# Six batches of queries on GpSimd's DMA queue, in place of keys cast by that queue: retention and a gated convolution on one core

## The chip, the cores and the metric

The kernel runs on one core of a Trainium2 chip. The metric is the time of one execution on the device in microseconds (us); the lower the better. The engines go by the profile's names: PE is TensorE (PEld its weight loads), DVE VectorE, ACT ScalarE, POOL GpSimd, SP SyncE. A DMA can be issued from SP's queue (the profile's "hardware_dynamic" q1) or from POOL's ("software_dynamic" q0); the same 16 DMA engines carry both.

## The reference

Inputs are q, k and v, each 8 batches x 8 heads x 576 tokens x 64 in f32, and the weights of a gated unit over 512 channels. The output is 8 x 576 x 512 in f32.

```python
# retention
scores = (1/sqrt(D)) * q @ k^T                        # per batch and head, 576 x 576
gamma  = 1 - 2 ** (-5 - h)
ret    = scores * where(i >= j, gamma[h] ** (i - j), 0)
attn   = ret @ v
# gated unit, on x = attn with the heads side by side (8 x 576 x 512)
gate   = sigmoid(sum over 5 taps of conv_w[tap] * x shifted by tap)   # causal, per channel
out    = (gate * (x @ w_val)) @ w_out
```

## The kernel before

The tokens are cut into 36 chunks of 128: in each half of the batches (four of them) 16 full chunks, four to a batch, and two "tail" chunks, each of the last 64 tokens of two batches. Within a chunk the scores are taken directly under a triangular mask; all earlier chunks of the batch come in through a running state (`state`, the sum of k^T v). The decay is split into a factor on v (`gin`, put on when v is rounded to bf16) and one on the result (`gout`).

The schedule is written out by hand: a loop over steps t from -2 to 37 emits each engine's instructions in the order in which that engine will run them. What one step emits for the change:

- `load(t + 6)`: DMA issues on SP's queue. `load_one` brings one chunk in f32, 256 KB in pieces of 256 B (64 floats of one head and token). Before the change it brings the values of every chunk, the keys of chunks 0 to 3 only, and the tails' own queries.
- `load_queries(b)`: one DMA of 1 MB on SP's queue for the queries of the four full chunks of batch b, in pieces of 1 KB (four tokens of one head), into the tile `fqb` of two buffers. Batches 0 and 1 are loaded ahead of the loop; for the others the step stands in `qload`.
- `load_keys(t + 6)`: a DMA on POOL's queue that reads 256 KB of f32 keys and writes 128 KB of bf16 straight into `kb`, which has 11 buffers; all chunks from the fifth (chunk 4) on go this way, chunk 4 ahead of the loop.
- `cast_v(t + 2)` (line 217): POOL multiplies the values by `gin` and rounds them, `vb`, four buffers. `cast_k` (line 212) rounds the first four chunks' keys, on DVE for chunks 0 and 1, on POOL for 2 and 3. `cast_q` (line 230) rounds one chunk's worth of queries on POOL, one step ahead of its transposition.
- TensorE's work of a step: `scores(t + 1)` (L275), `values(t)` (L316), `turn_k(t + 2)`, which transposes the keys (L237, read from `kb`), `turn_q` (L237 from `qb`), for every second step the convolution (L380) and the value product (L395), for the others the output projection (L406), and at the end `carried(t + 1)` (L299) and `update(t + 1)` (L347), the state update, which reads `kb` and `vb`.
- In odd steps SP issues two output DMAs (line 412), each of which waits for ACT's copy out of PSUM (line 409). SP issues in order, so what comes behind waits too.

Of the kernel before, what the change touches and what calls it, by code (L numbers as in the profile page):

```python
# [13 lines left out]
F32 = mybir.dt.float32  # L14
BF16 = mybir.dt.bfloat16
# [6 lines left out]
def kernel(  # L22
# [10 lines left out]
    nc = tc.nc  # L33
    B, H, S, D = q.shape
    DM = moe_w_val.shape[0]
    KC = moe_conv_w.shape[0]
    P = 128
    NP = H // 2
    NCH = S // P
    TAIL = S - NCH * P  # L40
    PAD = KC - 1
    GB = 4
    LA = 8
    RQ = NCH
# [5 lines left out]
    half = ctx.enter_context(tc.tile_pool(name="half", bufs=2))  # L50
    bfp = ctx.enter_context(tc.tile_pool(name="bfp", bufs=4))
# [12 lines left out]
    chunks = []  # L64
# [4 lines left out]
    NT = len(chunks)  # L69

    with tc.manual_schedule():
# [3 lines left out]
        def load_one(name, src, kind, b, c, bufs):  # L75
            t = half.tile([P, H, D], F32, name=f"f{name}c", bufs=bufs)
            if kind == "full":
                nc.sync.dma_start(out=t, in_=src[b, :, c * P:(c + 1) * P, :].rearrange("h p d -> p h d"))  # L78
            else:
                for i in range(2):  # L80
                    nc.sync.dma_start(out=t[i * TAIL:(i + 1) * TAIL],
                                      in_=src[b + i, :, c * P:S, :].rearrange("h p d -> p h d"))
            loaded[name, kind, b, c] = t

        def load(t):
            kind, b, c = chunks[t]
            if t < NCH:
                load_one("k", k, kind, b, c, NCH)
            if kind == "tail":
                load_one("q", q, kind, b, c, 2)  # L90
            load_one("v", v, kind, b, c, LA + 1)

        def load_keys(t):

            kind, b, c = chunks[t]
            kb = bfp.tile([P, H, D], BF16, name="kb", bufs=LA + 3)
            if kind == "full":
                nc.gpsimd.dma_start(out=kb, in_=k[b, :, c * P:(c + 1) * P, :].rearrange("h p d -> p h d"))  # L98
            else:
                for i in range(2):  # L100
                    nc.gpsimd.dma_start(out=kb[i * TAIL:(i + 1) * TAIL],
                                        in_=k[b + i, :, c * P:S, :].rearrange("h p d -> p h d"))
            kbf[t] = kb

        kbf, vbf = {}, {}

        def load_queries(b):
            t = half.tile([P, H, RQ, D], F32, name="fqb", bufs=2)
            nc.sync.dma_start(out=t.rearrange("p h r d -> p h (r d)"),
                              in_=q[b, :, 0:RQ * P, :].rearrange("h (p r) d -> p h (r d)", r=RQ))  # L110
            loaded["qb", b] = t

        cwn = consts.tile([KC * NP, P], F32, name="cwn")
        nc.scalar.dma_start(out=cwn, in_=moe_conv_w.rearrange("k (o i) -> (k o) i", i=P))
        load_one("k", k, *chunks[0], NCH)
        load_queries(0)
        load_one("v", v, *chunks[0], LA + 1)
        load(1)
# [60 lines left out]
        nc.vector.tensor_tensor(id2, ident[:, 0:64], ident[:, 64:128], op=ALU.add)  # L179
        mask_t = consts.tile([P, P], BF16, name="maskt")  # L180

        load_keys(NCH)

        wvb = consts.tile([P, NP, NP, P], BF16, name="wvb")
        wob = consts.tile([P, NP, DM], BF16, name="wob")
        dg = consts.tile([P, NP, KC, 64], BF16, name="dg")
# [20 lines left out]
            copy(wob[:, o], wof[:, o])  # L207


        def cast_k(t):  # L210
            kb = bfp.tile([P, H, D], BF16, name="kb", bufs=LA + 3)
            (nc.vector if t < 2 else nc.gpsimd).tensor_copy(kb, loaded["k", *chunks[t]])  # L212
            kbf[t] = kb

        def cast_v(t):
            vb = bfp.tile([P, H, D], BF16, name="vb")
            nc.gpsimd.tensor_tensor(vb, loaded["v", *chunks[t]],  # L217
                                    gin[:, chunks[t][2], :].unsqueeze(2).to_broadcast([P, H, D]), op=ALU.mult)
            vbf[t] = vb
# [4 lines left out]
        def cast_q(job, eng=nc.gpsimd):  # L224
            qb = bfp.tile([P, H, D], BF16, name="qb", bufs=5)
            if job[0] == "own":
                src = loaded["q", *chunks[job[1]]]
            else:
                src = loaded["qb", job[1]][:, :, job[2], :]
            eng.tensor_copy(qb, src)  # L230
            qbf[job] = qb
# [10 lines left out]
        def turn_k(t):  # L242
            ps = turned(kbf[t])
            kt = tp_sb.tile([P, NP, P], BF16, name="kt")
            nc.vector.tensor_copy(kt, ps)  # L245
            ktd[t] = kt

        def turn_q(job, copy=nc.scalar.copy, pool=None):
            ps = turned(qbf[job], pool)
            if job[0] == "own":  # L250
                qt = tp_sb.tile([P, NP, P], BF16, name="qt")
                qtd["own", job[1]] = qt
                dst = qt
            else:
                b, r = job[1:]
                if r == 0:
                    qtd["batch", b] = tp_sb.tile([P, NP, RQ, P], BF16, name="qtb", bufs=2)
                dst = qtd["batch", b][:, :, r, :]
            copy(dst, ps)  # L259
# [126 lines left out]
        def gate(n, i):  # L386
            t = gp.tile([P, 2, 2 * P], F32, name=f"gate{i}")
            nc.scalar.activation(t, gps[n][i], AF.Sigmoid)  # L388
            gsb[n].append(t)
# [28 lines left out]
        ok = lambda t: 0 <= t < NT  # L418
# [9 lines left out]
        qload = {}  # L428
        for b in range(2, B):
            first = min(s for s in qjobs if ("batch", b, 0) in qjobs[s])  # L430
            qload.setdefault(max(0, first - LA + 2), []).append(b)

        v_copy, g_copy, s_copy = nc.vector.tensor_copy, nc.gpsimd.tensor_copy, nc.scalar.copy
        for t in range(-2, NT + 2):
            n = t // 2 - 1
            unit = 0 <= n < NT // 2
            odd = t % 2 == 1
            jobs = qjobs.get(t, [])
            if t == -2:

                cast_k(0)
                turn_k(0)
                for s in sbl:
                    nc.vector.memset(s, 0.0)
                for r in range(RQ):
                    cast_q(("batch", 0, r), nc.vector if r % 2 else nc.gpsimd)
                cast_v(0)
                for r in range(RQ):
                    turn_q(("batch", 0, r), s_copy if r % 2 else v_copy, ps_g if r < 3 else None)
                warm = consts.tile([P, 1], F32, name="warm")  # L450
                nc.scalar.activation(warm, lsc, AF.Sigmoid)
                continue
            for b in qload.get(t, []):
                load_queries(b)
            if t >= 0 and ok(t + LA - 2):
                load(t + LA - 2)
            if ok(t + 2) and t == -1:
                cast_k(t + 2)
            if ok(t + 2):
                cast_v(t + 2)  # L460
            if t == -1:
                prep_wv(g_copy, 0)
            if t + 3 < NCH:
                cast_k(t + 3)
            if t >= -1 and NCH <= t + LA - 2 < NT:
                load_keys(t + LA - 2)
            for job in qjobs.get(t + 1, []):
                cast_q(job)
            if ok(t):
                take_state(t)  # L470
            if ok(t + 1):
                scores(t + 1)
                masks(t + 1, 0)
            if ok(t):
                values(t)
                if not odd:
                    take_x(t)
            if ok(t + 1) and not odd:
                masks(t + 1, 1)
            if unit and not odd:  # L480
                conv(n)
                gate(n, 0)
                gate(n, 1)
            if ok(t + 2) and not 1 <= t <= 3:
                turn_k(t + 2)
            if ok(t) and odd:
                take_x(t)
            if ok(t + 1) and odd:
                masks(t + 1, 1)
            if t == -1:  # L490
                prep_conv_weights()
            early = jobs if not 1 <= t <= 3 else []
            if unit:
                project(n, 0) if odd else value(n, 0)
            for job in early:
                turn_q(job)
            if unit:
                project(n, 1) if odd else value(n, 1)
            if ok(t + 2) and 1 <= t <= 3:
                turn_k(t + 2)  # L500
                for i, job in enumerate(jobs):
                    turn_q(job, v_copy if i % 2 else s_copy)
            if ok(t + 1):
                carried(t + 1)
                update(t + 1)
            if -1 <= t <= 0:
                prep_diagonals(2 * t + 2)
                prep_diagonals(2 * t + 3)
            if t == 1:
                prep_wv(s_copy, 1)  # L510
            if t == 2:
                for o in range(NP):
                    prep_wo(s_copy if o % 2 else v_copy, o)
                nc.gpsimd.tensor_copy(mask_t, mask)
                nc.gpsimd.memset(mask_t[0:64, 64:128], 0.0)
# [29 lines left out]
```

## Time and profile before

| | us |
|---|---|
| times of three runs | 176.56, 177.33, 178.78 |
| median | 177.33 |
| the profiled execution's own time | 176.56 |
| its span in the profile | 174.7 |

| engine | busy us | share of the span |
|---|---|---|
| PE | 150.4 | 86% |
| DVE | 117.7 | 67% |
| POOL | 94.1 | 54% |
| ACT | 88.4 | 51% |

| DMA issued | from | count, KB each | median us to landing |
|---|---|---|---|
| `fqb` (queries of a batch) | SP | 8 x 1024 | 9.0 |
| `fvc` (values of a full chunk) | SP | 32 x 256 | 6.9 |
| `fkc` (keys of the first chunks) | SP | 4 x 256 | 6.8 |
| `kb` (keys, cast; bytes written) | POOL | 28 x 128 and 8 x 64 | 7.2 and 4.6 |
| output | SP | 32 x 256 | 4.2 |

The profile comes from one execution, and the span is the part of its time from the first to the last thing that the profiler saw. Busy time is a mean over a start of some 24 us, in which the first loads arrive, and a steady run after it. "L98" is line 98 of the kernel. A DMA engine can work on packets of two queues at once, so shares of DMA time can add to more than 100%. In the lines of an engine in order of time, the numbers are the start and the length in us, and in brackets the idle time before and what ended it; in the list of waits they are the total, the number and the longest.

### The profile page before, as it was taken

The numbers are of one execution on the slowest core, as the hardware profiler recorded it, in microseconds if no ns is written. First come the engines' busy times: TensorE is split into PE (matmuls) and PEld (weight loads), VectorE is DVE, ScalarE is ACT, GpSimd is POOL, SyncE is SP. The second block draws the span as 40 slices with busy tenths as digits, with TensorE's granted clock in tenths as the row PEclk, the third lists the DMA queues.
The fourth block names the chain that finished last, engine by engine and source line by source line (L and its number), as shares of the span: only waits on it lengthen the run. The fifth ranks groups of instructions, "written<-read, shape, count | busy, mean of one in ns | idle before, by whom it ended". The sixth has DMA issues, their size and how long they took to land.

```text
span 174.7 us, 5491 instructions
## 1 busy us (share of the span) xinstructions
PE 150.4 (86%) x2273; PEld 111.9 (64%) x2273; DVE 117.7 (67%) x229; ACT 88.4 (51%) x180; POOL 94.1 (54%) x123
## 2 busy tenths in 40 slices
PE   0275359489999999999999999999999999999980
PEld 0154247357786868677686868677786867777630
DVE  6667813476767777776867777776866788776330
ACT  6361412175566565647454565647475554545330
POOL 7256257469994597825970795578575243100000
PEclk9999999999999999999999999999999999999998
DMA  5999999999999999999999999999999991303114
GB/s 136 279 293 249 219 261 233 298 283 221 249 292 254 226 223 199 283 183 294 178 271 237 220 300 244 198 246 203 161 185 123 230 219 64 120 4 123 71 50 120
DMA packets 93957, 36.00 MB, mean 206 GB/s; under 512 B 80090, under 2 KB 88302, under 8 KB 93934
## 3 DMA queue, kind: packets, MB, share of 16 engines
q1 hardware_dynamic: 60400, 31.20, 70.2%
q0 software_dynamic: 33344, 4.20, 37.7%
q8 instruction: 17, 0.28, 0.7%
q10 hardware_dynamic: 190, 0.27, 0.6%
q14 instruction: 6, 0.05, 0.1%
HBM read 30.42 MB, written 9.44 MB: 228 GB/s over the span
## 4 chain that ended last, share of the span: by engine, by line
PE 80%; SPq 9%; DMA 4%; DVE 2%; ACT 1%; issue 1%; POOL 0%; ACTq 0%; DVEq 0%
PE g L395 19%; PE g L406 17%; PE g L380 13%; PE tps L237 11%; PE o L316 7%; PE s L275 6%; SPq L78 4%; DMA fkc<-in_k_dram 4%; PE st L347 4%; SPq L125 3%; PE o L299 3%; SPq L121 1%; DVE z L398 1%; ACT qtb L259 1%; ACT ob L409 1%
## 5 line engine op out<-in xcount | busy, mean ns | idle before, releaser
L217 POOL TENSOR_TENSOR vb<-fvc,gin 128x512 bf16<-128x512 f32 x36 | 37.6, 1045 | 36.2 <-DMA fvc<-in_v_dram 12.8
L284 DVE TENSOR_TENSOR p<-s,maskq 128x512 bf16<-128x512 f32 x64 | 43.8, 685 | 15.1 <-PE s L275 14.9
L398 DVE TENSOR_TENSOR z<-gate,g 128x512 bf16<-128x512 f32 x36 | 24.8, 688 | 20.9 <-PE g L395 20.9
L395 PE MATMUL g<-xg,wvb 128*128 128x256 bf16 x288 | 37.4, 276 | 0.0
L406 PE MATMUL g<-wob,z 128*128 128x512 bf16 x144 | 36.3, 379 | 0.3 <-DVE z L398 0.3
L409 ACT COPY ob<-g 128x512 f32<-128x512 f32 x36 | 21.1, 586 | 25.7 <-PE g L406 25.5
L388 ACT ACTIVATE gate<-g 128x512 f32<-128x512 f32 x36 | 19.5, 594 | 20.0 <-PE g L380 20.0
L395 PEld LDWEIGHTS <-wvb 128*128 128x128 bf16 x288 | 27.0, 99 | 3.7 <-issue 0.8
L98 POOL DMA_DIRECT2D kb<-in_k_dram x28 | 26.6, 948 | 0.0
L358 ACT CAST sbd<-st 64x256 bf16<-64x256 f32 x48 | 17.6, 367 | 16.6 <-PE st L347 16.1
L237 PE MATMUL tps<-ident,kb 128*128 128x128 bf16 x144 | 15.1, 231 | 11.1 <-POOL kb L212 6.5
L380 PE MATMUL g<-xg,dg 64*64 64x256 bf16 x720 | 24.3, 279 | 0.0
L230 POOL CAST qb<-fqb 128x512 bf16<-128x512 f32 x30 | 19.1, 643 | 8.6 <-DMA fqb<-in_q_dram 8.6
L326 DVE TENSOR_TENSOR xg<-o,gout 128x512 bf16<-128x512 f32 x32 | 21.7, 680 | 0.0
L259 ACT COPY qtb<-tps 128x512 bf16<-128x512 bf16 x27 | 15.9, 589 | 9.2 <-PE tps L237 9.2
L380 PEld LDWEIGHTS <-dg 64*64 64x64 bf16 x720 | 19.0, 109 | 2.3 <-issue 0.6
L406 PEld LDWEIGHTS <-z 128*128 128x128 bf16 x144 | 12.6, 98 | 10.6 <-DVE z L398 1.3
L237 PEld LDWEIGHTS <-kb 128*128 128x128 bf16 x144 | 8.8, 101 | 16.4 <-POOL kb L212 7.0
L245 DVE COPY kt<-tps 128x512 bf16<-128x512 bf16 x36 | 15.2, 424 | 5.8 <-PE tps L237 5.6
L237 PEld LDWEIGHTS <-qb 128*128 128x128 bf16 x144 | 11.3, 103 | 10.9 <-issue 3.9
L237 PE MATMUL tps<-ident,qb 128*128 128x128 bf16 x132 | 13.0, 222 | 3.3 <-DVE kt L245 1.5
L316 PE MATMUL o<-p,vb 128*64 128x128 bf16 x288 | 15.6, 232 | 0.0
(60 smaller groups left out, 128.9 us busy)
## 6 DMA issues: line engine op xcount, KB each, us to landing
fqb<-in_q_dram SPq DMA_DIRECT2D x8, 1024.0 KB, 9.0
fvc<-in_v_dram SPq DMA_DIRECT2D x32, 256.0 KB, 6.9
out_dram<-ob SPq DMA_DIRECT2D x32, 256.0 KB, 4.2
kb<-in_k_dram POOLq DMA_DIRECT2D x28, 128.0 KB, 7.2
fkc<-in_k_dram SPq DMA_DIRECT2D x4, 256.0 KB, 6.8
wvf<-in_moe_w_val_dram SPq DMA_DIRECT2D x1, 1024.0 KB, 7.5
wof<-in_moe_w_out_dram SPq DMA_DIRECT2D x4, 256.0 KB, 6.0
fqc<-in_q_dram SPq DMA_DIRECT2D x8, 128.0 KB, 4.4
```

Of the source, the lines that this page charges most:

```text
L98: nc.gpsimd.dma_start(out=kb, in_=k[b, :, c * P:(c + 1) * P, :].rearrange("h p d -> p h d"))
L217: nc.gpsimd.tensor_tensor(vb, loaded["v", *chunks[t]], gin[:, chunks[t][2], :].unsqueeze(2).to_broadcast([P, H, D]), op=ALU.mult)
L237: nc.tensor.transpose(ps[:, pr, :], flat[:, pr * P:(pr + 1) * P], ident)
L284: nc.vector.tensor_tensor(p, sps[t][i], m.unsqueeze(1).to_broadcast([P, NP, P]), op=ALU.mult)
L316: nc.tensor.matmul(o[r, pr, :], lhsT=vb[:, 2 * pr + i, :], rhs=pt[t, i][:, pr, :], start=(fresh and pr == 0), stop=(pr == NP - 1), skip_gr ...
L326: nc.vector.tensor_tensor(by_token(x[:, bl, :, PAD + i0:PAD + i0 + P]), ops[t].rearrange("p o (r n) -> p o n r", r=RQ), by_token(gout[:, : ...
L380: nc.tensor.matmul(g[bank][cols, pr, :], lhsT=dg[rows, blk, kk, :], rhs=xs(n, rows, blk, kk), start=(pr == 0 and kk == 0), stop=(pr == 1 a ...
L388: nc.scalar.activation(t, gps[n][i], AF.Sigmoid)
L395: nc.tensor.matmul(vps[:, j, :], lhsT=wvb[:, o, 2 * i + j, :], rhs=xs(n, slice(0, P), o, PAD), start=(j == 0 and o == 0), stop=(j == 1 and ...
L398: nc.vector.tensor_tensor(z, gsb[n][i], vps, op=ALU.mult)
L406: nc.tensor.matmul(o, lhsT=zsb[n, j // 2][:, j % 2, i * P:(i + 1) * P], rhs=wob[:, j, :], start=(j == 0), stop=(j == NP - 1))
L409: nc.scalar.copy(ob, o)
```

## The change

Keys of all chunks now come in f32 on SP's queue, through `load_one` into a tile of 9 buffers, and are rounded by `cast_k` on POOL three steps ahead (on DVE still for chunks 0 and 1), into `kb` with the pool's four buffers. `load_keys` is gone. The batch-wise queries go into three buffers in place of two; batches 0 and 1 still come on SP's queue ahead of the loop, and the six others are issued from POOL's queue, without a cast: batch 2's at step 0 as before, the others' two steps later in the loop than before (`first - LA + 4`; batch 3's at step 3).

```diff
         def load(t):
             kind, b, c = chunks[t]
-            if t < NCH:
-                load_one("k", k, kind, b, c, NCH)
+            load_one("k", k, kind, b, c, LA + 1)
             if kind == "tail":
                 load_one("q", q, kind, b, c, 2)
             load_one("v", v, kind, b, c, LA + 1)
 
-        def load_keys(t):
-            kind, b, c = chunks[t]
-            kb = bfp.tile([P, H, D], BF16, name="kb", bufs=LA + 3)
-            if kind == "full":
-                nc.gpsimd.dma_start(out=kb, in_=k[b, :, c * P:(c + 1) * P, :].rearrange("h p d -> p h d"))
-            else:
-                for i in range(2):
-                    nc.gpsimd.dma_start(out=kb[i * TAIL:(i + 1) * TAIL],
-                                        in_=k[b + i, :, c * P:S, :].rearrange("h p d -> p h d"))
-            kbf[t] = kb
...
         def load_queries(b):
-            t = half.tile([P, H, RQ, D], F32, name="fqb", bufs=2)
-            nc.sync.dma_start(out=t.rearrange("p h r d -> p h (r d)"),
+            t = half.tile([P, H, RQ, D], F32, name="fqb", bufs=3)
+            (nc.sync if b < 2 else nc.gpsimd).dma_start(out=t.rearrange("p h r d -> p h (r d)"),
                               in_=q[b, :, 0:RQ * P, :].rearrange("h (p r) d -> p h (r d)", r=RQ))
             loaded["qb", b] = t
...
-        load_keys(NCH)
...
         def cast_k(t):
-            kb = bfp.tile([P, H, D], BF16, name="kb", bufs=LA + 3)
+            kb = bfp.tile([P, H, D], BF16, name="kb")
             (nc.vector if t < 2 else nc.gpsimd).tensor_copy(kb, loaded["k", *chunks[t]])
             kbf[t] = kb
...
-            qload.setdefault(max(0, first - LA + 2), []).append(b)
+            qload.setdefault(max(0, first - LA + 4), []).append(b)
...
-            if t + 3 < NCH:
+            if ok(t + 3):
                 cast_k(t + 3)
-            if t >= -1 and NCH <= t + LA - 2 < NT:
-                load_keys(t + LA - 2)
```

In the order of POOL's instructions the issue of a batch's queries stands behind the query cast of the step before and ahead of a value cast; the first of the six stands between the cast of keys 2 and the values of chunk 2. The order on PE, ACT and DVE is the same as before.

More of the change, by code (lines that the diff above doesn't have):

```diff
@@ L91, in load @@
             load_one("v", v, kind, b, c, LA + 1)
-        def load_keys(t):
-            kind, b, c = chunks[t]
-            kb = bfp.tile([P, H, D], BF16, name="kb", bufs=LA + 3)
-            if kind == "full":
-                nc.gpsimd.dma_start(out=kb, in_=k[b, :, c * P:(c + 1) * P, :].rearrange("h p d -> p h d"))
-            else:
-                for i in range(2):
-                    nc.gpsimd.dma_start(out=kb[i * TAIL:(i + 1) * TAIL],
-                                        in_=k[b + i, :, c * P:S, :].rearrange("h p d -> p h d"))
-            kbf[t] = kb
-        kbf, vbf = {}, {}
         def load_queries(b):
-            t = half.tile([P, H, RQ, D], F32, name="fqb", bufs=2)
-            nc.sync.dma_start(out=t.rearrange("p h r d -> p h (r d)"),
+            t = half.tile([P, H, RQ, D], F32, name="fqb", bufs=3)
+            (nc.sync if b < 2 else nc.gpsimd).dma_start(out=t.rearrange("p h r d -> p h (r d)"),
                               in_=q[b, :, 0:RQ * P, :].rearrange("h (p r) d -> p h (r d)", r=RQ))
@@ L114 @@
         nc.scalar.dma_start(out=cwn, in_=moe_conv_w.rearrange("k (o i) -> (k o) i", i=P))
-        load_one("k", k, *chunks[0], NCH)
+        load_one("k", k, *chunks[0], LA + 1)
         load_queries(0)
@@ L207, in prep_wo @@
             copy(wob[:, o], wof[:, o])
+        kbf, vbf = {}, {}
         def cast_k(t):
-            kb = bfp.tile([P, H, D], BF16, name="kb", bufs=LA + 3)
+            kb = bfp.tile([P, H, D], BF16, name="kb")
             (nc.vector if t < 2 else nc.gpsimd).tensor_copy(kb, loaded["k", *chunks[t]])
```

## The prediction

> **What bounds the kernel now.** I read the page's slices and chain first, then the waits of TensorE, then the order of time on POOL and TensorE, and last the DMA packets of short stretches.
>
> ```profile
> PE   0275359489999999999999999999999999999980
> ...
> DMA  5999999999999999999999999999999991303114
> ...
> PE 80%; SPq 9%; DMA 4%; DVE 2%; ACT 1%; issue 1%; POOL 0%; ACTq 0%; DVEq 0%
> ```
>
> A slice is 4.4 us. From slice 10 on TensorE is full to the end, and the chain that ended last is 80% TensorE; what it has of SP's queue (9%) and DMA (4%) lies before 24 us. But the DMA engines are full too, up to about 140 us. So TensorE sets the end, with the transfers close behind. The waits of TensorE tell how close:
>
> ```profile
> PE tps L237 <- POOL kb L212: 6.5, 2, 4.6
> ...
> PE g L406 <- DVE z L398: 0.3, 1, 0.3
> ```
>
> The longest is one wait of 4.6 us for a key cast. In order of time that is chunk 3:
>
> ```profile
> 23.16 0.61 POOL L212 CAST kb<-fkc 128x512 bf16<-128x512 f32 x1 [4.18 <-DMA fkc<-in_k_dram]
> ...
> 28.19 2.28 POOL L230 CAST qb<-fqb 128x512 bf16<-128x512 f32 x4 [1.12 <-DMA fqb<-in_q_dram]
> ...
> 31.01 0.39 PE L237 MATMUL tps<-ident,kb 128*128 128x128 bf16 x4
> ...
> 110.70 1.04 POOL L217 TENSOR_TENSOR vb<-fvc,gin 128x512 bf16<-128x512 f32 x1 [3.34 <-DMA fvc<-in_v_dram]
> ...
> 116.52 0.40 PE L237 MATMUL tps<-ident,kb 128*128 128x128 bf16 x4
> ```
>
> Chunk 3's keys land at 23.1 us and TensorE starts its unbroken run at 23.8. At 28.1 us batch 1's queries land. At 31.01 TensorE turns the keys of chunk 4. Values of chunk 25 (the 26th row of L217) land at 110.7, and the keys of that chunk are turned at 116.52, its values used in the state update at 123.6: the transfers run some 6 to 13 us ahead of TensorE, no more. Two chunks take TensorE about 8 us (one L380 group to the next, 104.06 to 111.87).
>
> The price of a packet, from three short stretches (9.8 to 10.4 us; 22.2 to 23.2; 117.5 to 119):
>
> ```profile
> DMA packets 527, 0.14 MB, mean 226 GB/s; under 512 B 526, under 2 KB 526, under 8 KB 527
> ...
> q0 software_dynamic: 480, 0.06, 93.4%
> q1 hardware_dynamic: 473, 0.12, 79.4%
> ...
> q0 software_dynamic: 679, 0.09, 90.2%
> q1 hardware_dynamic: 979, 0.25, 76.4%
> ```
>
> Alone, SP's queue moves 527 packets of 256 B in 0.6 us: 878 per us, 1024 packets (one chunk) in 1.17 us. Beside GpSimd's casting queue it moves 473 per us, or 979 in 1.5 us (653 per us). Each cast packet thus cost it (878 - 473) / 480 = 0.84 packet, or (878 - 653) / (679 / 1.5) = 0.50. A casting load of one key chunk costs the engines 0.6 to 1.0 us of SP's queue, less than the plain load of the same chunk.
>
> **The change part by part.** Taken out of POOL: 28 issues at L98 of 0.94 us and 8 at L101 of 0.71 us, 32 us. Put in: 32 casts of keys at 0.61 us (the L212 row on POOL), 19.6 us, and six issues of query loads. No plain 1 MB issue stands on POOL; the nearest rows are L98's 0.94 us, also 1024 pieces, and SP's shortest for the same tile, 0.39 us; I take 0.94, 5.6 us, ends 2.3 and 5.6. POOL gets lighter by 7 to 10 us. I count this as nothing: POOL is busy 54%, and with four value buffers it may run two chunks (8 us) ahead of TensorE, while its work for a chunk is 1.04 + 0.61 + 0.62 = 2.27 us. That cover also hides the new dependence that a key is cast in POOL's order, and that kb has 4 buffers in place of 11.
>
> The Trainium skill's SBUF — State Buffer, section SBUF: two separate sides, warns that a DMA issued from GpSimd waits for its descriptors while VectorE runs an operation that takes both ports, and gives 3.1 us in place of 0.62 us. L98's 28 issues took 937 to 1085 ns beside a VectorE that is 67% busy, so the measurement shows no such wait here; by the page's difference six loads would hold POOL an estimated 15 us longer in all.
>
> SP's queue loses six query loads (1 MB; 1.35 us median to issue) and gains 28 loads of 256 KB and 8 of 128 KB of keys. SP issues in order, and its longer issues are times in which the ring behind it is full (0.39 to 2.93 us for the same L78 load), so what counts is engine time:
> - Keys: 32 chunks x 1.17 us plain, less 32 x (0.6 to 1.0) casting: +5 to +18 us.
> - Queries: 1 MB in packets of 1 KB took SP's queue 3.05 us at the 344 GB/s of 25.5 to 27 us. Issued by GpSimd it may cost all of this, or as little as half, as the cheaper cast packets did: 0 to -9 us for six.
> - Sum: -4 to +18 us; the middles, +11.5 and -4.5, give +7 us, over 32 chunks 0.22 us each.
>
> What hides it: the lead. At chunk 25 the values landed at 110.7, the keys would be one load (1.2 us) earlier, 109.5; 22 chunks at 0.22 make it 114.3; with 0.65 us for the cast 115.0, and TensorE wants it at 116.5. It holds by 1.5 us in the middle of the bounds. At the upper end, 0.56 each, it is 122.5 and TensorE is 6 us late; at the lower end there is nothing to gain, since TensorE has no gap there. At chunk 22 (values landed at 99.53, keys turned at 105.28) the same sum gives 103.2: 2 us left. SP's pauses for output tiles between 41 and 110 us, some 9 us, take up a part besides. I take +0.4 us here, bounds 0 and +6.
>
> The start is the other place. The load of keys 4 from POOL (issued at 3.11 us) goes: 1024 x (0.50 to 0.84) packets, 0.6 to 1.0 us earlier for all behind it. In its place the queries of batch 2 are issued by POOL right after the cast of keys 2, about 16.5 us, with no wait since there are three buffers; before, SP issued them at 24.84, behind the values of chunk 5. In the before, POOL's load of 16.49 moved its packets only around 22 us, so of batch 2's 3 us I put half before keys 3 at most: keys 3 land at 23.1 - 0.8 + (0 to 1.5), TensorE starts -0.8 to +0.7 us. Were the 1 MB served wholly ahead, it is +2.2. Next in SP's queue are values 3, queries 1 (28.1), and now keys 4: 28.1 + 1.2 - 0.8 (keys 4) - 0.8 (keys 5, also gone from GpSimd's queue) + (1.5 to 3.05) = 29.2 to 30.8, cast by 29.9 to 31.5 against 31.01. Behind that cast on POOL wait the four casts of queries 1 (0.57 us each); TensorE takes them 0.9 to 1.1 us apart, so they stay ahead. Keys 5 land 2.4 us later, about 32.4, and are wanted at 38.7. I take +0.3 us, bounds -0.8 and +2.2.
>
> Sum: +0.3 + 0.4 = +0.7 us on the profiled execution's own 176.56 us (span 174.7 and 1.86 around it), 177.3. That execution is the lowest of three; their median is 177.33, and on it the sum gives 178.0, which is my figure. Bounds: -0.8 and +8.2, that is 176.5 to 185.5.
>
> **The rivals.**
> *The transfers take over* (slower). If a plain key chunk costs more over a casting one than 0.3 us net of what the queries save, the lead of 6 us is used up near chunk 20 to 25 and TensorE waits at L237 for POOL's key cast. For it: DMA is at 9 in all slices up to 140 us, and POOL waits for values ten times, 12.8 us in all. Against it: SP pauses for output tiles, so the rings are not always short of time. Half of the upper bound, +3 us, to all of it, +6, and +0.7 at the start: median 181 to 184, I take 182.
>
> *The start wins* (faster, under the bound of 2%). Keys 3 come 0.8 us earlier, batch 2's queries flow later, and the lead holds: 176.5. For it: POOL's earlier load came out 5 us after its issue. It is no way to gain more: after 36 us TensorE has waits of under 1 us in all, so a gain of over 3.5 us has no place except in keys 3 landing 3.5 us earlier, which nothing removed is worth.
>
> *The query loads come late.* They now have three chunks' time, 12 us, from issue to cast on POOL's queue; the landing took 9.0 us median on SP's, and GpSimd's took 7.2 for an eighth of the bytes written. If it takes 18 us POOL, which runs two chunks ahead less its 2.3 us of work, makes TensorE wait: 0.5 us or so each, six times, +3: 181.
>
> **How the numbers follow.** Within 2% (3.5 us, about what a measurement of this kernel can tell from no change) lie my forecast, 0.50, and the winning start, 0.13, which give 0.63. The transfers taking over has 0.24 and late queries 0.07, mostly beyond +3.5 us: slower 0.31. I leave 0.06 for a gain over 2% that I have no mechanism for. The likeliest's own range is 176.5 to 180; the range given reaches to most of the transfers' case, 176 to 183.5.
>
> **What would show it.** Right: TensorE's run starts at 23 to 24.5 us; after it L237 waits for kb under 1 us in all; POOL holds 34 key casts near 0.61 us and six query issues near 0.94; GpSimd's queue holds 6 MB; packets of 256 B on SP's queue rise by some 32,800. Wrong: waits of L237 for POOL's key casts after 60 us (transfers), waits for query casts (late queries), a second slow stretch of matmuls after a pause at keys 4, or vb waiting for fvc past TensorE's need.

## The result and the profile after

The changed kernel takes 185.11 us (median of four, 184.83 to 185.59) against 177.43 us (median of four): 1.0428 times as long, 95% interval 1.0359 to 1.0498. It is slower by 4%, above the range of the prediction (176 to 183.5) and a little inside the sum of its bounds (185.5). One execution of one experiment below (the 40 fillers) was disturbed throughout and is left out.

The page of the changed kernel, in slices of 4.6 us:

```profile
PE   0277092554899999999999999999999999999990
...
POOL 5349120994249454491467369448565434400000
PEclk9999999555599999999999999999999999999999
...
PE 74%; SPq 10%; DMA 6%; DVE 4%; ACT 1%; issue 1%; POOL 1%; ACTq 0%; DVEq 0%; POOLq 0%
```

TensorE is full from the twelfth slice on and stays so to the end, as before. The fifth slice, with nothing, is the wait for keys 3, which the kernel before has too. What is new lies behind it: four slices at less than 6 tenths (the seventh to the tenth), and the granted clock, a row of nines before but for the last slice, at 5 in the eighth to the eleventh. The list of waits has it too:

```profile
PE tps L222 <- POOL kb L197: 9.4, 3, 4.3
...
PE g L391 <- DVE wob L190: 4.0, 1, 4.0
```

A third wait for a key cast has come in (9.4 us in place of 6.5), and 4.0 us for VectorE's rounding of w_out (`wob`). TensorE in order of time:

```profile
22.89 0.61 PE L222 MATMUL tps<-ident,kb 128*128 128x128 bf16 x4 [4.26 <-POOL kb L197]
...
32.62 0.55 PE L222 MATMUL tps<-ident,kb 128*128 128x128 bf16 x4 [3.86 <-POOL kb L197]
...
43.83 3.57 PE L391 MATMUL g<-wob,z 128*128 128x512 bf16 x8 [3.98 <-DVE wob L190]
...
50.17 1.29 PE L365 MATMUL g<-xg,dg 64*64 64x256 bf16 x40
```

The first line is keys 3 (23.82 us before), the second keys 4 (31.01), the third the first output projection (36.95), the last the convolution of step 4 (40.80). From that convolution on the two kernels are the same to the hundredth: the thirteenth such group behind it starts at 152.73 us here and at 143.36 before, 102.56 us later in both. So the difference of the two profiles lies between 22 and 50 us (0.3 us of it come back behind the last matmul):

| from | to | before us | after us | difference |
|---|---|---|---|---|
| start | keys 3 turned | 23.82 | 22.89 | -0.93 |
| keys 3 | keys 4 turned | 7.19 | 9.73 | +2.54 |
| keys 4 | output projection | 5.94 | 11.21 | +5.27 |
| output projection | convolution of step 4 | 3.85 | 6.34 | +2.49 |
| sum | | 40.80 | 50.17 | +9.37 |

(The profiled execution of before is the fastest of its runs and that of after the slowest, so the medians differ by less, 7.7 us.)

Three things happen there. *Keys 4 come late.* POOL's queue and SP's queue between 23 and 25 us:

```profile
DMA packets 289, 0.68 MB, mean 341 GB/s; under 512 B 129, under 2 KB 131, under 8 KB 289
...
q0 software_dynamic: 159, 0.65, 96.6%
q1 hardware_dynamic: 130, 0.03, 9.5%
```

In 2 us POOL's megabyte of batch 2 moved 0.65 MB and SP's queue 0.03 MB. The packets tell why: 159 against 130, about one for one, but POOL's are of 4 KB (0.65 MB over 159) and SP's of 256 B. On POOL, in order of time:

```profile
15.95 1.06 POOL L94 DMA_DIRECT2D fqb<-in_q_dram  x1
...
22.22 0.61 POOL L197 CAST kb<-fkc 128x512 bf16<-128x512 f32 x1 [3.80 <-DMA fkc<-in_k_dram]
26.59 1.04 POOL L202 TENSOR_TENSOR vb<-fvc,gin 128x512 bf16<-128x512 f32 x1 [3.76 <-DMA fvc<-in_v_dram]
31.95 0.61 POOL L197 CAST kb<-fkc 128x512 bf16<-128x512 f32 x1 [4.32 <-DMA fkc<-in_k_dram]
```

Batch 2 is issued at 15.95 us, keys 3 land at 22.2 (0.9 us earlier than before), values 3 at 26.6 (1.5 us later), keys 4 at 31.9. TensorE had ended its work at 28.7 us. With batch 2 on SP's queue (an experiment below) the cast of keys 4 starts at 28.10 us, 3.85 earlier.

*The clock halves.* Stretches of the changed kernel (start and end, length, busy time of PE with its instructions, then the other engines; then granted clock, DMA share, GB/s):

```profile
28.70:32.60 3.90, 0.06 (x1) 0.00 (x0) 0.69 (x1) 0.00 (x0) 0.65 (x2) 1.00 0.92 178
32.60:39.80 7.20, 4.80 (x44) 3.59 (x45) 2.72 (x4) 2.94 (x6) 7.12 (x13) 0.51 1.20 219
39.80:43.80 4.00, 0.05 (x2) 0.08 (x1) 4.00 (x2) 0.00 (x0) 3.69 (x6) 0.50 1.05 312
43.80:50.20 6.40, 5.85 (x40) 2.97 (x40) 2.80 (x6) 2.38 (x5) 0.78 (x2) 0.53 0.87 188
```

TensorE does nothing from 28.7 to 32.6 us and then works at 0.50 to 0.53 until 50. Counted so, the slow clock is 1.29 us of the third row of the table (5.27 less the wait of 3.98) and all of the last; at full clock the wait of 3.98 would have been longer.

*VectorE's rounding of w_out takes 5.5 us.* VectorE and POOL in the changed kernel:

```profile
37.29 0.92 POOL L94 DMA_DIRECT2D fqb<-in_q_dram  x1
...
38.23 1.05 POOL L202 TENSOR_TENSOR vb<-fvc,gin 128x512 bf16<-128x512 f32 x1
38.27 5.85 DVE L190 CAST wob<-wof 128x512 bf16<-128x512 f32 x2
...
41.88 0.60 POOL L215 CAST qb<-fqb 128x512 bf16<-128x512 f32 x1
42.46 1.03 POOL L202 TENSOR_TENSOR vb<-fvc,gin 128x512 bf16<-128x512 f32 x1
43.83 1.01 PE L391 MATMUL g<-wob,z 128*128 128x512 bf16 x2 [3.98 <-DVE wob L190]
```

The two casts together took 0.75 us before. Here the first lasts 5.51 us and ends 0.3 us behind a row of POOL casts that ran without a pause from 38.23 to 43.49. TensorE's projection waits for it.

### The profile page after: what moved, and what is told of

Same layout as the page of the kernel before. It is cut to its first block, busy times and chain, and to the rows that moved or that the text cites. A ratio compares the mean times of both kernels' runs of the same rounds, so it can differ in the third digit from the quotient of the medians.

```text
span 183.8 us, 5590 instructions
## 1 busy us (share of the span) xinstructions
PE 153.4 (83%) x2273; PEld 113.3 (62%) x2273; DVE 122.8 (67%) x229; ACT 88.4 (48%) x180; POOL 86.9 (47%) x125
## 4 chain that ended last, share of the span: by engine, by line
PE 74%; SPq 10%; DMA 6%; DVE 4%; ACT 1%; issue 1%; POOL 1%; ACTq 0%; DVEq 0%; POOLq 0%
PE g L391 17%; PE g L380 16%; PE g L365 11%; PE tps L222 11%; DMA fkc<-in_k_dram 6%; PE o L301 6%; PE s L260 6%; SPq L78 5%; PE st L332 4%; DVE wob L190 3%; SPq L110 3%; PE o L284 3%; SPq L94 2%; ACT qtb L244 1%; ACT ob L394 1%
## 5 line engine op out<-in xcount | busy, mean ns | idle before, releaser
L197 POOL CAST kb<-fkc 128x512 bf16<-128x512 f32 x34 | 20.7, 609 | 54.5 <-DMA fkc<-in_k_dram 24.2
L391 PE MATMUL g<-wob,z 128*128 128x512 bf16 x144 | 38.0, 393 | 4.3 <-DVE wob L190 4.0
L380 PE MATMUL g<-xg,wvb 128*128 128x256 bf16 x288 | 36.7, 273 | 0.0
L394 ACT COPY ob<-g 128x512 f32<-128x512 f32 x36 | 21.1, 585 | 31.8 <-PE g L391 31.5
L365 PE MATMUL g<-xg,dg 64*64 64x256 bf16 x720 | 23.5, 273 | 0.0
L391 PEld LDWEIGHTS <-z 128*128 128x128 bf16 x144 | 13.0, 100 | 15.6 <-issue 5.8
L215 POOL CAST qb<-fqb 128x512 bf16<-128x512 f32 x30 | 18.6, 628 | 4.1 <-DMA fqb<-in_q_dram 4.1
L365 PEld LDWEIGHTS <-dg 64*64 64x64 bf16 x720 | 18.5, 107 | 2.1 <-issue 0.6
L222 PEld LDWEIGHTS <-qb 128*128 128x128 bf16 x144 | 12.1, 108 | 10.7 <-POOL qb L215 3.9
L222 PE MATMUL tps<-ident,qb 128*128 128x128 bf16 x132 | 14.0, 234 | 2.9 <-ACT qtb L244 1.3
```

The lines of the kernel that those rows point to most:

```text
L222: nc.tensor.transpose(ps[:, pr, :], flat[:, pr * P:(pr + 1) * P], ident)
L365: nc.tensor.matmul(g[bank][cols, pr, :], lhsT=dg[rows, blk, kk, :], rhs=xs(n, rows, blk, kk), start=(pr == 0 and kk == 0), stop=(pr == 1 a ...
L380: nc.tensor.matmul(vps[:, j, :], lhsT=wvb[:, o, 2 * i + j, :], rhs=xs(n, slice(0, P), o, PAD), start=(j == 0 and o == 0), stop=(j == 1 and ...
L391: nc.tensor.matmul(o, lhsT=zsb[n, j // 2][:, j % 2, i * P:(i + 1) * P], rhs=wob[:, j, :], start=(j == 0), stop=(j == NP - 1))
L394: nc.scalar.copy(ob, o)
```

## The experiments

Theory A stands for these three things; theory B for the transfers as the limit, which was the slower rival of the prediction. Ratios are to the kernel before, on the same chip, with 95% intervals.

**w_out rounded on ScalarE.**

```diff
-                    prep_wo(s_copy if o % 2 else v_copy, o)
+                    prep_wo(s_copy, o)
```

> The changed kernel with all four roundings of w_out on ScalarE in place of two on VectorE. Theory A (three links at the start: keys 4 come late, TensorE idles 3.9 us and its clock halves, and VectorE's rounding of w_out is held 5.5 us because GpSimd runs its casts without a pause): TensorE's wait of 4.0 us at L391 goes, and with it part of the 2.5 us that the slow clock costs behind it: 179.2 us, 178.5 to 181.2. Theory B (the transfers are the limit, and TensorE waits for whatever comes last): no change, 184.5 to 185.5.

Measured: 179.32 us, ratio 1.0107 (1.0056 to 1.0157). The wait at L391 is gone, and TensorE reaches the convolution of step 4 at 44.71 us in place of 50.17. So the 4.0 us and the slow clock behind them are worth 5.8 us of the 7.7; the transfers are the same in both kernels.

**Batch 2 on SP's queue.**

```diff
-            (nc.sync if b < 2 else nc.gpsimd).dma_start(...)
+            (nc.sync if b < 3 else nc.gpsimd).dma_start(...)
```

> The changed kernel, but batch 2's queries are issued from SP's queue at step 0 again (batches 3 to 7 from GpSimd). Theory A: batch 2's megabyte stands behind keys 5 and values 5 again, keys 4 land near 28.6 us in place of 31.9, TensorE waits for them under 1 us and keeps its clock; GpSimd waits for batch 2's queries near 36 us, so the rounding of w_out on VectorE takes 0.42 us; all of the loss goes: 176.5 us, 175.5 to 178. Theory B: keys still travel plain, so most of the loss stays: 182 to 185.

Measured: 180.18 us, ratio 1.0139 (1.0083 to 1.0195). The start came out as theory A has it: keys 4 are turned at 29.62 us with no wait, w_out takes 0.75 us, and the convolution of step 4 is at 40.78 us (40.80 before). But the time did not follow. TensorE in this run, behind 60 us:

```profile
93.22 0.40 PE L222 MATMUL tps<-ident,kb 128*128 128x128 bf16 x4 [0.20 <-POOL kb L197]
...
103.53 0.40 PE L222 MATMUL tps<-ident,kb 128*128 128x128 bf16 x4 [2.40 <-POOL kb L197]
```

Between the convolutions of steps 16 and 20 this kernel loses 2.9 us (88.36 to 106.92, against 88.38 to 104.06 before), waiting for POOL's key casts, and these for keys: before the cast that ends at 103.5 POOL had waited 4.92 us for them. So the transfers do bind in this kernel, as theory B has it. The changed kernel starts 9.4 us later, and its keys are there. But that the late start is the reason is not shown: the run with batch 2 from POOL one step later (below) starts 0.9 us earlier than this one, and its profile has no such wait.

**The queries' part alone** (keys as in the kernel before).

```diff
-            t = half.tile([P, H, RQ, D], F32, name="fqb", bufs=2)
-            nc.sync.dma_start(...)
+            t = half.tile([P, H, RQ, D], F32, name="fqb", bufs=3)
+            (nc.sync if b < 2 else nc.gpsimd).dma_start(...)
...
-            qload.setdefault(max(0, first - LA + 2), []).append(b)
+            qload.setdefault(max(0, first - LA + 4), []).append(b)
```

> The kernel before with only the queries' part of the change (six loads from GpSimd's queue, three buffers, two steps later); keys are still cast by GpSimd's queue. Theory A: keys 4 are there from 9 us on, so TensorE does not idle 3.9 us and keeps its clock; but GpSimd no longer waits for batch 2's queries, so it may run through when VectorE rounds w_out: 177 us if its DMA issues leave VectorE a gap, 181 if not. Theory B: fewer plain packets than in the changed kernel, about as many as before: 177 us.

Measured: 180.7 us, ratio 1.0218 (1.0141 to 1.0295). Near the second number, but by another way. Keys 4 are there, yet the queries of batch 1 are now late: TensorE waits 2.81 us for their cast at 33.5 us, and the clock is at half from 35 to 42. w_out takes 0.84 us: it falls beside POOL's small mask operations and a DMA issue. The convolution of step 4 is at 44.38 us and nothing is lost behind it. This run has both kinds of packets on POOL's queue, first the keys cast on the way (21 to 23 us), then batch 2 (25 to 27 us):

```profile
q0 software_dynamic: 965, 0.12, 99.2%
q1 hardware_dynamic: 881, 0.22, 80.1%
```

```profile
q0 software_dynamic: 156, 0.64, 94.1%
q1 hardware_dynamic: 92, 0.06, 11.6%
```

The counts of the two queues are within 10% of each other the first time and within a factor of 1.7 the second (156 and 92, 52 of these of 1 KB), while the sizes differ far more. What SP's queue gets goes mostly by the size of a packet: 0.22 MB of 0.34 beside casts of 128 B, 0.06 of 0.70 beside 4 KB.

**The keys' part alone** (all queries on SP's queue, two buffers, old steps).

```diff
-            t = half.tile([P, H, RQ, D], F32, name="fqb", bufs=3)
-            (nc.sync if b < 2 else nc.gpsimd).dma_start(...)
+            t = half.tile([P, H, RQ, D], F32, name="fqb", bufs=2)
+            nc.sync.dma_start(...)
...
-            qload.setdefault(max(0, first - LA + 4), []).append(b)
+            qload.setdefault(max(0, first - LA + 2), []).append(b)
```

(against the changed kernel)

> The changed kernel with only the keys' part (all keys plain on SP's queue and rounded on GpSimd); all queries on SP's queue at the old steps in two buffers. Theory A: as with batch 2 alone on SP's queue, 176.5 us, 175.5 to 178. Theory B: the plain keys cost the engines 0.2 to 0.6 us a chunk and nothing is taken off SP's queue: 183 to 186.

Measured: 178.02 us (ten runs), ratio 1.0060 (1.0018 to 1.0101). The convolution of step 4 comes at 40.07 us, 0.7 earlier than before, and three waits for keys (1.32, 0.57 and 1.68 us, between 85 and 104 us) take back more than that in the profiled execution (179.65 us, the slowest but one of the ten). With the run before: by their intervals the keys' part costs 0.3 to 1.8 us net and the queries' part alone 2.5 to 5.2; together they cost 7.7, since only together do keys 4 wait behind batch 2 and does POOL run a row of casts when VectorE rounds w_out.

**w_out rounded one step earlier**, still half on VectorE.

```diff
+            if t == 1:
+                for o in range(NP):
+                    prep_wo(s_copy if o % 2 else v_copy, o)
             if t == 2:
-                for o in range(NP):
-                    prep_wo(s_copy if o % 2 else v_copy, o)
```

> The changed kernel, with the rounding of w_out (two quarters on VectorE, two on ScalarE) one step earlier, near 24 us, where GpSimd waits for values 3; the DMA engines are as full there. Theory A: VectorE's two casts take 0.42 us each and TensorE does not wait for them: 179.3 us, 178.5 to 180.5, as with ScalarE. If VectorE's cast was slow from the transfers and not from GpSimd, it takes several us there as well and TensorE starts its convolution later: 182 to 186.

Measured: 179.77 us (ten runs), ratio 1.0091 (1.0048 to 1.0135). VectorE's casts run at 25.13 us and take 0.75 us together, with POOL idle from 24.1 to 27.7 and the DMA engines full. So it is not the transfers that hold them.

**POOL's row cut short**, by fewer buffers for the rounded values (four in the changed kernel).

```diff
-            vb = bfp.tile([P, H, D], BF16, name="vb")
+            vb = bfp.tile([P, H, D], BF16, name="vb", bufs=3)   # and 2 in the second run
```

> The changed kernel with three buffers for the rounded values in place of four, so that GpSimd runs one chunk less ahead. Theory A: GpSimd's row that began at 38.2 us and ended at 43.5 ends near 42.4, where its seventh values wait for TensorE, and VectorE's rounding of w_out ends 1 us earlier with it: 184 us, 183 to 185. If the row is not the cause: the rounding keeps its 5.5 us and the time stays at 185 or is more.

> The changed kernel with two buffers for the rounded values. Theory A: GpSimd has to wait for TensorE's use of values 3 (39.9 us) before it can round values 5, so the row breaks at 38.2 us, VectorE's rounding of w_out takes 0.42 us and TensorE's wait at L391 goes: near 180 us at the start's account, plus what the missing lead costs in the steady run, which may be several us; the length of the rounding decides, not the time. If the row is not the cause: 5.5 us again.

Measured: 184.42 us (182.92 and 185.93) and 181.40 us (180.34 and 182.46), two runs each. VectorE's casts with three buffers, POOL's last two casts of the row, and the shortest, median and longest of VectorE's two casts in ns with their first and last start; then with two buffers:

```profile
37.33 5.26 DVE L190 CAST wob<-wof 128x512 bf16<-128x512 f32 x2
...
40.95 0.60 POOL L197 CAST kb<-fkc 128x512 bf16<-128x512 f32 x1
41.50 0.80 POOL L215 CAST qb<-fqb 128x512 bf16<-128x512 f32 x1
...
L190 DVE CAST wob<-wof x2: 829/2668/4508, 37.3 to 41.8; 128x512 bf16<-128x512 f32 x2
```

```profile
37.26 0.93 POOL L94 DMA_DIRECT2D fqb<-in_q_dram  x1
...
37.61 1.13 DVE L190 CAST wob<-wof 128x512 bf16<-128x512 f32 x2
```

With three buffers the row has six POOL instructions in place of seven and ends at 42.3 us in place of 43.5. The cast that is held takes 4.51 us in place of 5.51 and ends at 41.84: 0.3 us behind the last but one of the row, and the last, at 0.80 us in place of 0.61, comes out longer for it. With two, POOL stops behind its DMA issue, the casts take 1.13 us in all and TensorE's wait is gone. So the cast waits as long as POOL's casts follow each other, and goes when they stop. This settles what holds it; that it can get in only at the end of the row is not so.

**The cost by itself**: one more rounding on VectorE in each of 20 steps.

```diff
+            if 8 <= t < 28:
+                nc.vector.tensor_copy(scr, wof[:, 0])
```

> The changed kernel with one more rounding of a quarter of w_out on VectorE in each of the steps 8 to 27, into a tile that is not read: the cost in dispute by itself. Theory A (VectorE's rounding waits as long as GpSimd runs one cast after the other): those that meet GpSimd idle or issuing a DMA take 0.42 us, those that meet a row of casts take what is left of it, 1 to 2.5 us, and end when GpSimd pauses. If GpSimd does not matter: 0.42 us, all twenty.

Measured (190.05 us, one run, with these casts in it):

```profile
L488 DVE CAST scr<-wof x20: 407/562/1255, 71.2 to 146.9; 128x512 bf16<-128x512 f32 x20
```

Nine of the twenty take less than 0.5 us, the others up to 1.25. POOL matters, but not as theory A said: where a cast here meets a row, it gets in at the end of the POOL instruction that is running (79.51 us, beside a key cast that ends at 79.98: done at 80.26), and the next POOL cast is the longer for it (0.81 us in place of 0.61). That is also how the cast got in with three buffers. The rounding of w_out in the same execution waited through a whole row again (5.79 us for two). Why it is passed over there, one POOL instruction after the other, stays open.

**Fillers**: transposes of the identity just ahead of those of keys 4 (on top of w_out on ScalarE; 40, and then 16).

```diff
+            if t == 2:
+                fill = ps_t.tile([P, NP, P], BF16, name="tps")
+                for i in range(40):
+                    nc.tensor.transpose(fill[:, i % NP, :], ident, ident)
```

> The run with w_out rounded on ScalarE, and 40 transposes of the identity put on TensorE just ahead of the transposition of keys 4 (their result is not read), so that TensorE is not idle while it waits for them. Theory A: with ScalarE's rounding alone the clock was 0.5 for some 7 us behind the wait and the convolution of step 4 came 3.9 us later than in the kernel before; if idleness is what halves it, the clock stays at 1.0 from 32 us on and 1.5 us come back: 177.8 us, 177.2 to 178.6. If the clock falls for another reason, the fillers only add up to 2 us: 179 to 181.

> The run with w_out rounded on ScalarE, with 16 transposes of the identity ahead of the transposition of keys 4 in place of 40, so that they take 0.9 us at full and 1.8 us at half clock, less than the wait of 2 to 4 us. If idleness halves the clock: 178 us, and the clock stays at 1.0 longer behind 32 us. If the clock falls in spite of them: 179.3, as without.

Measured: with 40, 179.42 to 180.84 us (ratio 1.0111, 1.0032 to 1.0191); with 16, 180.47 us (179.53 and 181.41). Neither is faster than the 179.32 us without. The clock of the second, and below it the same stretches without fillers:

```profile
32.00:36.00 4.00, 1.55 (x16) 1.14 (x17) 0.85 (x2) 1.13 (x3) 4.00 (x8) 0.94 1.00 212
36.00:40.00 4.00, 3.90 (x32) 2.50 (x32) 2.31 (x4) 2.75 (x7) 3.92 (x8) 0.50 1.30 230
```

```profile
32.00:36.00 4.00, 2.16 (x16) 1.59 (x17) 0.85 (x2) 0.59 (x1) 4.00 (x8) 0.54 1.07 223
36.00:40.00 4.00, 3.33 (x31) 2.19 (x30) 1.70 (x4) 3.29 (x7) 3.92 (x8) 0.50 1.27 218
```

The fillers keep the clock for 32 to 36 us, 0.94 in place of 0.54, and it is lost in the next 4 us all the same: between 32 and 36 TensorE is busy 1.55 us of 4, since the four query transpositions there wait for copies. So a stretch with little work does go before the fall; but this place of the schedule has two such stretches, and filling the first saves nothing. The run with batch 2 on SP's queue, where no single wait in this stretch is over 1 us, has the same fall: 0.62 over 34.2 to 38.7 us, behind a stretch with 1.78 us busy of 4.6. Yet the kernel before has that stretch too, 1.77 us busy of 4.6 between 31.0 and 35.6 us, and its clock stays at 1.00 behind it. So little work alone doesn't bring the fall. In the traces the halved clock lasts a multiple of 3.41 us (3.41 with batch 2 on SP's queue, 10.24 with w_out on ScalarE, 17.07 in the changed kernel), so it may depend on where a stretch lies in such a period; no run tests that, and the cause of the fall stays open.

**Batch 2 from POOL one step later**, w_out on ScalarE.

```diff
-            qload.setdefault(max(0, first - LA + 4), []).append(b)
+            qload.setdefault(max(1, first - LA + 4), []).append(b)
```

> The run with w_out rounded on ScalarE, and GpSimd's load of batch 2's queries one step later (behind the cast of keys 3, near 22.8 us). Theory A: its megabyte then moves behind keys 4, which land near 28.6 us, and the start is as in the kernel before or 1 us earlier. What is left is what the transfers cost later on, which the late start hid: with batch 2 on SP's queue TensorE waited 2.9 us for keys between 88 and 107 us. So 178 to 180.5 us; 176.3 if the transfers cost nothing; 179.3 or more if keys 4 are late all the same.

Measured: 177.92 us (ten runs, 175.19 to 178.81), ratio 1.0011 (0.9961 to 1.0060). The start is 1 us better than before (convolution of step 4 at 39.85), and in the profiled execution, the fastest, TensorE waits for no keys later; what the others, up to 3.6 us longer, lose, no trace shows. So with two small edits all of the change's loss goes; there is no gain to be measured.

**The first loads in another order**: w_out behind keys 3, values 3 and the queries of batch 1, in the kernel before and then in the last one.

```diff
-        wo_src = ...
-        for (...): nc.sync.dma_start(out=wof[...], in_=wo_src[ab, hl])
         load(3)
         load_queries(1)
+        wo_src = ...
+        for (...): nc.sync.dma_start(out=wof[...], in_=wo_src[ab, hl])
```

> The kernel before, with the load of w_out (1 MB, four DMAs) moved behind keys 3, values 3 and the queries of batch 1 on SP's queue. If the order of the first loads is what sets the start, keys 3 land near 17.5 us in place of 23.1 and the time falls by 2 to 5 us: 174 us, 172 to 176, less what the transfers then cost later. If the start is set elsewhere: 177.2.

> The changed kernel with w_out rounded on ScalarE, batch 2's queries issued by GpSimd one step later, and the load of w_out behind the queries of batch 1. Theory A: both early faults gone and the first keys earlier, as in the kernel before with that load moved (174.7 us): 173 to 175.5 us. If the plain keys then leave TensorE waiting, because the transfers have less of a lead: 176 to 179.

Measured: in the kernel before 174.66 us, ratio 0.9790 (0.9716 to 0.9863), faster than both kernels. Keys 3 are cast at 18.4 us in place of 23.2, and the convolution of step 4 is at 38.79; part of the 5 us goes to waits behind. In the other kernel 181.68 us, ratio 1.0203 (1.0027 to 1.0379), a miss:

```profile
33.43 0.61 PE L222 MATMUL tps<-ident,kb 128*128 128x128 bf16 x4 [7.69 <-POOL kb L197]
```

There keys 4 come on SP's queue too, behind w_out now; they are cast at 32.8 us, TensorE stands for 7.7 us, and the clock halves. I had moved the load ahead of the one piece that this kernel needs next. And as keys 3 come early, so does POOL's issue of batch 2 behind their cast (18.14 us), so that its megabyte stands ahead of keys 4 as well. It is the fault of the change once more: whatever stands in front of keys 4 decides the start.

## Why the prediction was wrong

- *Steady run: right that TensorE sets it, and that it pays nothing.* I took +0.4 us; it is 0.00 over 102.56 us. But the account of the lead that was to hide the plain keys is not confirmed. The runs with batch 2, or all queries, on SP's queue lose 2.9 and 3.8 us between 80 and 107 us, which lies in my bounds (0 to +6) and not at the value taken. The changed kernel is spared, and so is the profiled execution with batch 2 a step later, which starts 10.3 us earlier; why these two and not the others stays open. One reading was off: SP's waits for output tiles between 41 and 110 us add up to 19.3 us in the list of waits (17.5 at L412, 1.8 at L415), not to some 9.
- *Keys 3: at the early end.* I had them 0.8 us earlier to 0.7 later; measured 0.9 earlier. Batch 2's packets begin at 21.5 us, 0.7 before keys 3 land.
- *Keys 4: the first step that failed.* I summed volumes, and gave batch 2 between 1.5 and 3.05 us of SP's time ahead of keys 4: cast by 29.9 to 31.5 us. The cast ended at 32.6. Measured against the run with batch 2 on SP's queue this term is 3.85 us (31.95 against 28.10), over my upper end, which had the whole megabyte ahead. The lower end was wrong in its reason: my prices for a packet beside POOL's queue (0.50 and 0.84) were read from packets of 128 B, and I carried them over to the queries as "as little as half". The packets of a plain load from POOL are of 4 KB, and while they run SP's queue nearly stands (0.03 of 0.68 MB in 2 us). What goes beyond the upper end does not look like volume: between 30.5 and 31.5 us the DMA share is 0.23 (44 GB/s), and keys 4 are still not complete. What holds their last packets stays open.
- *POOL at nothing: the step that cost most (4.0 us of waiting at L391).* "I count this as nothing", since POOL was busy 54% and its work had a cover of 8 us. That was an argument about what waits for POOL's results. It left out who shares something with POOL while it runs. In the kernel before POOL happened to wait for batch 2's queries (until 36.50 us) as VectorE rounded w_out (36.14 to 36.9). The change made these queries early and POOL's casts more, and the pause went. I read the Trainium skill's SBUF — State Buffer only for descriptors. Its section Who interferes with whom says that a VectorE copy or cast in a 2-port mode and a GpSimd instruction block each other, and that the one that comes first holds the ports for its whole instruction. The runs agree on the block; the wait is longer than one instruction of the other engine: 5.5 us, seven POOL instructions, for w_out. The extra casts, up to 1.25 us, waited for one.
- *The clock: named as a sign, not priced.* "A second slow stretch of matmuls after a pause at keys 4" is what came, worth 3.8 us in the profile (1.29 and 2.49). The trace of before had the price: its matmuls at the start took 0.61 us in groups that later took 0.39, though its granted clock reads 1.00 there.
- *The rivals.* The transfers' rival named a time close to the measured one (181 to 184) by a mechanism that did not act; its sign, waits for key casts after 60 us, is absent. Late queries did not come up in the changed kernel: POOL's six issues take 0.92 to 1.06 us, as assumed, and its waits for batch queries are those of the first load alone (4.1 us, once).

## What to carry to other kernels

A load moved to another queue is not only moved in time: ask what its packets weigh against those that it will meet, and put nothing large on a second queue while the first brings what the next engine waits for. When an engine's work moves "under cover", look at which other engine's operations until now fell into its pauses. And read the start of a kernel apart from its steady run: here both kernels are the same to the hundredth behind 50 us, and a better order of the first loads is worth more (2.1%) than either version of the steady run.

## What the runs showed of the hardware that was not expected

- Two DMA queues shared the engines more nearly by packets than by bytes: 965 to 881 (128 B against 256 B), 159 to 130 (4 KB against 256 B) and 156 to 92 (4 KB against 256 B and 1 KB), so the second split was 0.65 to 0.03 MB.
- A VectorE f32 to bf16 cast of 128x512, 0.42 us alone, took 5.5 us beside a row of seven GpSimd instructions and ended 0.3 us behind the row; with the row shortened by one instruction it took 4.5 us and got in ahead of the last, and with POOL stopped the two together took 1.13 us. Extra casts in the steady run waited for one GpSimd instruction only.
- TensorE's granted clock fell to half behind stretches in which it was busy under 40% (1.78 of 4.6 us, 1.55 of 4), with no single wait over 1 us in the first case, and stayed there for 3.41 us or a multiple of it. Behind the same stretch in the kernel before (1.77 of 4.6 us) it did not fall.
